# Moving the sum of the value squares to the end of its step, and halving GpSimd's subtractions

## Chip, cores and metric

One Trainium2 chip, one core. The metric is the device time of one execution in microseconds (us). Before the change it is 759.63 us, the median of 3 runs (757.01 to 761.63).

## What is computed

Attention over 8 batches, 8 heads, 576 positions and 64 values per head, then a mixture of eight experts with a fixed capacity of 576 tokens each. Heads 0 to 3 see a band of 32 positions, heads 4 to 7 see every 32nd position:

```python
scores = scale * np.matmul(q, k.transpose(0, 1, 3, 2))
mask_local = (rel >= 0) & (rel < stride)
mask_strided = (rel >= 0) & (pos[None, :] % stride == pos[:, None] % stride)
scores = np.where(masks[None, :, :, :], scores, -1000000000.0)
attn = softmax(scores)              # with 1e-09 in the divisor
x = np.matmul(attn, v)              # as 4608 tokens of 512
logits = x @ w_gate                 # each token goes to one expert, greedily, 576 per expert
out[mask] = np.maximum(x[mask] @ w1[e], 0.0) @ w2[e]
```

## The kernel before

**Stages.** The first some 260 us of the span are attention and gating, then follows a search for the assignment of tokens to the first expert, and then the eight experts, each with its gather of tokens, its weights and its scatter. The change lies in the first stage.

**Units and steps.** A batch has two units, first the strided heads, then the local ones, so unit j is batch j // 2; a unit has two pairs of heads. The program runs over steps i = -1 to 31, and the tile framework keeps each engine's instructions in the order in which the program writes them (`manual_schedule`). In step i three pairs are in work: `u` is pair i (its probabilities are multiplied by the values, `mix`, and the result is divided and scaled, `norm`), `n` is pair i + 1 (its scores are closed, its maxima are taken with `max_main` and `max_t`, then `shift` subtracts them on TensorE, line 387, and ScalarE takes the exponential, line 391), and `m` is pair i + 2 (its scores are opened). So on TensorE one step runs: close scores of n (line 364), mix of head 0 of u (408), maxima (374), mix of head 1 (408), open scores of m (353, 364), transposes of earlier results (`flip`, 482), and last the shift of n (387). I call the time from one shift to the next the length of a step.

**The scale of a batch.** The results are kept as two 16-bit halves, so each batch gets a power of two as a scale, from the sum of the squares of its values. ScalarE squares the values of a unit with a running sum per partition (`square_v`, line 299) into two columns of `vsq`. `total_v` sums them over the partitions on TensorE with a matrix of twos (line 302, 2 columns) into the small PSUM area `b`, and VectorE adds the two columns to `vsum` (304). `scale_v` makes two powers of two from it with four small VectorE instructions (`scale_of`, lines 203 to 208) and writes the exponent into the table `val` (311 and 313). `norm` of that batch needs the scale (line 429), except in the first unit, which is scaled afterwards.

**Where the sum stands.** For batches 1 to 7 total_v and scale_v are in the list `mids` of step 4b, the step whose u is the first pair of the batch's strided unit. `mids` runs between the two mixes. The square of the local unit is queued on ScalarE at the end of the step before (4b - 1), at the front of the list `fills`; the third argument of `at`, `True`, puts it there already in this kernel, ahead of `finish`. For batch 0 the sum stands in step 1 behind the norm. The list `mids3`, behind the norm and the flips, holds the logits of batch b - 2 in step 4b (line 562).

**Finish.** A pair's result x is cut into its upper half by ScalarE (line 444) and its lower half by GpSimd (x minus the upper half, line 445, both operands in SBUF), for later flips and for the stores to the scratch memory, which SyncE issues (460, 468).

```python
            def total_v(u, po):
                nc.tensor.matmul(po[:, :2], twos, vscale[u.b][0], start=True, stop=True, skip_group_check=True)
                u.vsum = wk.tile([128, 1], F32, name="vsum")
                nc.vector.tensor_reduce(u.vsum, po[:, :2], axis=AX.X, op=OP.add)
```

Of the kernel before, what the change touches and what calls it, by code (L numbers as in the profile page):

```python
# [13 lines left out]
OP = mybir.AluOpType  # L14
AX = mybir.AxisListType
# [44 lines left out]
V_BITS, W1_BITS, W2_BITS = 8, 7, 15  # L60
# [72 lines left out]
def band_stride_attention_then_capacity_moe(ctx, tc, qt, kl, ks, nl, ns, wg, w1, w2, cst, out, dbg=None):  # L133
    nc = tc.nc
# [39 lines left out]
    twos = const.tile([128, 128], F32, name="twos")  # L174
# [26 lines left out]
    def scale_of(tot, bits, pool, sc=None):  # L201
        ex = pool.tile([128, 3], I32, name="ss_e", bufs=3)
        nc.vector.tensor_single_scalar(ex[:, 2:3], tot.bitcast(I32), 24, op=OP.logical_shift_right)
        nc.vector.tensor_scalar(ex[:, 0:1], ex[:, 2:3], -1.0, float(127 + bits + 63), op0=OP.mult, op1=OP.add)
        nc.vector.tensor_scalar(ex[:, 1:2], ex[:, 2:3], 1.0, float(127 - bits - 63), op0=OP.mult, op1=OP.add)
        if sc is None:
            sc = pool.tile([128, 2], I32, name="ss_s", bufs=3)
        nc.vector.tensor_single_scalar(sc, ex[:, :2], 23, op=OP.logical_shift_left)  # L208
        return sc.bitcast(F32), ex

    def spans(b):
        n0 = b * S
        c0 = n0 // TP
        half, full = (slice(0, 64), c0 + 4) if n0 % TP == 0 else (slice(64, 128), c0)
        t0 = 0 if n0 % TP == 0 else 64
        c1 = c0 if t0 == 0 else c0 + 1
        return [(slice(0, TP), c1 + i, slice(t0 + i * TP, t0 + i * TP + TP)) for i in range(4)] + \
            [(half, full, slice(S - 64, S) if t0 == 0 else slice(0, 64))]

    with tc.tile_pool(name="ld", bufs=2) as ld, \  # L220
# [8 lines left out]
        mxb, vbuf, vscale = {}, {}, {}  # L229
# [7 lines left out]
        b = spare[:, 1, 384:]  # L237
        nc.vector.memset(po_all, 0.0)
        for i in range(2):
            for g in "sl":  # L240
                t = ld.tile([128, 32], F32, name=f"mx_{g}{i}", bufs=1)
                nc.gpsimd.memset(t, 0.0)
                mxb[g, i] = t
                t = ld.tile([128, 2, ST if g == "s" else LT, 4, VW], F32, name=f"v_{g}{i}", bufs=1)
# [29 lines left out]
        class Unit:  # L274
# [24 lines left out]
                    nc.scalar.activation(jk[r], u.vn[r, g, :, :, :D], AF.Square, accum_out=vscale[u.b][0][r, j:j + 1])  # L299

            def total_v(u, po):
                nc.tensor.matmul(po[:, :2], twos, vscale[u.b][0], start=True, stop=True, skip_group_check=True)
                u.vsum = wk.tile([128, 1], F32, name="vsum")
                nc.vector.tensor_reduce(u.vsum, po[:, :2], axis=AX.X, op=OP.add)

            def scale_v(u):
                b = u.b
                sv, ex = scale_of(u.vsum, V_BITS, wk)
                sp = spans(b)
                c = sp[0][1]  # L310
                nc.vector.tensor_scalar(val[:, 2, c:c + 4], ex[:, 1:2].to_broadcast([TP, 4]), 1.0, None, op0=OP.mult)
                r, c, _ = sp[4]
                nc.vector.tensor_scalar(val[r, 2, c:c + 1], ex[r, 1:2], 1.0, None, op0=OP.mult)
                vscale[b] = sv, None

            def load(u, parts=(slice(0, 2),), v=True):
                b, g = u.b, u.g
# [120 lines left out]
            def finish(u, p, eng):  # L438
                nr, nx = u.nr, u.nx
                if p == 0:  # L440
                    u.xo = wk.tile([128, nx, 2, 4 * D], F16, name="xo" + u.g)
                xf = u.x[:nr, :, 2 * p:2 * p + 2].rearrange("q t h d -> q t (h d)")
                c = slice(2 * D * p, 2 * D * p + 2 * D)
                nc.scalar.activation(u.xo[:nr, :, 0, c], xf, AF.Copy)  # L444
                eng.tensor_tensor(u.xo[:nr, :, 1, c], xf, u.xo[:nr, :, 0, c], op=OP.subtract)  # L445

            def store(u):
                b, xo = u.b, u.xo.rearrange("q t j d -> q t (j d)")
# [126 lines left out]
        todo = [Unit(b, strided) for b in range(B) for strided in (True, False)]  # L575
# [9 lines left out]
        mids2, mids3 = {1: todo[1]}, {GW_AT: [lambda a, b: gate_weights(b)]}  # L585
        mids, flips = {}, {}

        for j, u in enumerate(todo):
            if j == 1:
                for k in range(6):  # L590
                    drips.setdefault(k // 3, []).append(lambda u=u, k=k: u.copy_v(k))
                for p in range(2):
                    drips.setdefault(2, []).append(lambda p=p: todo[0].rescale(p))
            if j > 1:
                if not u.strided:
                    for k in range(6):
                        drips.setdefault(2 * j + COPY_AT[k], []).append(lambda u=u, k=k: u.copy_v(k))
                    at(2 * j - V_AT, u.square_v, True)
                else:
                    for f in range(2):  # L600
                        at(2 * j + 2 - V_AT_S[f], lambda u=u, f=f: u.square_v(f), j > 2)
                if not u.strided:
                    mids.setdefault(2 * j - 2, []).append(lambda a, b, u=u: (u.total_v(b), u.scale_v()))
            if not u.strided and u.b < B - 1:
                at(2 * j + (4 if u.b < B - 2 else 3), lambda k=u.b: gate_scale(k))
                if u.b < B - 2:
                    mids.setdefault(2 * j + G_AT, []).append(lambda a, b, k=u.b: gates(k, spare))
                (mids if u.b == B - 2 else mids3).setdefault(2 * j + (G_AT + 1 if u.b < B - 2 else 5), []).append(lambda a, b, k=u.b: logits(k, b))
            for p in range(2):
                at(2 * j + p if j else 2, lambda u=u, p=p: u.finish(p, nc.gpsimd))  # L610
            at(2 * j + (2 if j < nu - 2 else 1), u.store)
            if j < nu - 2:
                for p in range(2):
                    k = 2 * j + p + (2 if j else 3)
                    flips.setdefault(k, []).append((u, p))
            elif u is not todo[-1]:
                at(2 * j + 1, u.turn)
# [35 lines left out]
        def warm(i, k):  # L653
            for _ in range(WARM.get((i, k), 0)):
                nc.tensor.matmul(warm_o, warm_i[:, :128], warm_i, start=True, stop=True, skip_group_check=True)
# [5 lines left out]
        for i in range(-1, 2 * nu):  # L661
            u, n, m = pair(i), pair(i + 1), pair(i + 2)
            if i > 0 and i % 2 == 0 and i // 2 + 3 < nu:
                todo[i // 2 + 3].load()
            if n:
                close_scores(n)
            warm(i, 0)
            for f in drips.get(i, []):
                f()
            if m or i in mids:  # L670
                a = room(m) if m else ps_a.tile([128, 2, 512], F32, name="spa")
            if u:
                if u[1] == 0:
                    u[0].begin()
                if i < last:
                    u[0].mix(u[1], 0)
            if i < last:
                for f in mids.get(i, []):
                    f(a, b)
            if i == last:  # L680
                gate_scale(B - 1)
                warm(i, 1)
                pt = ps_a.tile([128, 2, 512], F32, name="spa")
                pt = pt[:, 0], pt[:, 1]
                p1 = spare[:, 0]
                for ts_, p_ in zip(parts, (None, p1)):
                    for h in range(2):
                        u[0].mix(u[1], h, ts_, p_)
                    u[0].norm(u[1], ts_, p_)
                break  # L690
            if n and MAX_FIRST:
                n[0].max_t(n[1])
            if u:
                u[0].mix(u[1], 1)
            if n and not MAX_FIRST:
                n[0].max_t(n[1])
            if i == last - 1:
                gates(B - 2, ps_a.tile([128, 2, 512], F32, name="spa"))
            warm(i, 1)
            if m:  # L700
                open_scores(m)
            warm(i, 2)
            if u:
                u[0].norm(u[1])
            for v, p in flips.get(i, []):
                v.flip(p)
                if len(flips[i]) > 1:
                    v.flipped(p)
            if i in mids2:
                mids2[i].total_v(b)  # L710
            if i == 1:
                todo[1].scale_v()
            for f in mids3.get(i, []):
                f(a, b)
            if i == -1:
                todo[0].square_v()
            if n:
                n[0].shift(n[1])
            warm(i, 3)
            if len(flips.get(i, [])) == 1:  # L720
                flips[i][0][0].flipped(flips[i][0][1])
            if i in (-1, 0):
                todo[1].square_v(i + 1)
            if i == 0:
                nc.scalar.activation(jkw, wg_sb, AF.Square, accum_out=sqw)
            for f in late.get(i, []) + fills.get(i, []):
                f()
# [659 lines left out]
```

## Time and profile before

| what | us |
|---|---|
| median of 3 runs | 759.63 (757.01 to 761.63) |
| the profiled execution's own time | 753.18 |
| its span in the profile | 751.2 |
| TensorE busy in the span | 655.4 (87%) |
| VectorE, ScalarE, GpSimd busy | 470.4, 357.1, 159.3 |

TensorE is in front, but its share is a mean over unlike stages; the profile also shows it at half clock for long stretches of the first stage. Rows of the timeline begin with the start in us from the span's start and the duration in us; then come the engine (PE is TensorE, PEld its weight loads, DVE VectorE, ACT ScalarE, POOL GpSimd, SP SyncE), the line, the operation, output and inputs, and in brackets the idle time before the row with what ended it.

### The profile page before, as it was taken

Reading aid. Unit: us, or ns where it says so; the run is one execution under the profiler, and the core shown is the slowest. Engines: PE = TensorE matmul, PEld = TensorE weight load, DVE = VectorE, ACT = ScalarE, POOL = GpSimd, SP = SyncE. Lnnn points to the kernel's source line nnn. Section 1 sums busy time; section 2 is a strip of 40 time slices with the busy share of each in tenths; the row PEclk is TensorE's granted clock in tenths of the full one; section 3 lists DMA queues with packets and bytes.
Section 4 is the critical chain, followed back from the end, with each engine's and each line's share of the span. In section 5 each row is a group of like instructions: output and inputs, shape, how many; then the busy total and the mean of one; then the engine's idle time right before and its main releaser. Section 6 shows DMA issues by size and latency. Waiting matters only on the chain.

```text
span 751.2 us, 18257 instructions
## 1 busy us (share of the span) xinstructions
PE 655.4 (87%) x7519; PEld 418.9 (56%) x7519; DVE 470.4 (63%) x1369; ACT 357.1 (48%) x548; POOL 159.3 (21%) x143
## 2 busy tenths in 40 slices
PE   5877889888698634899999999999999998899994
PEld 3555557666475532654664754764754753564752
DVE  5866676565667767796766775676775764653210
ACT  3445675554645403547527436436436335754210
POOL 9131131121212402005005004004005004112011
PEclk9668997687979856999999999999999999799998
DMA  9975575554612305419229149049049049651001
GB/s 233 261 212 129 148 205 160 159 157 135 200 33 65 77 20 195 116 48 307 61 94 289 33 141 248 26 149 252 15 166 235 15 165 242 233 125 50 15 22 42
DMA packets 75695, 102.89 MB, mean 137 GB/s; under 512 B 43020, under 2 KB 52788, under 8 KB 75100
## 3 DMA queue, kind: packets, MB, share of 16 engines
q1 hardware_dynamic: 68812, 82.23, 38.8%
q0 software_dynamic: 6080, 19.10, 8.2%
q8 instruction: 59, 0.97, 0.6%
q10 hardware_dynamic: 720, 0.39, 0.2%
q14 instruction: 24, 0.20, 0.1%
HBM read 73.59 MB, written 18.87 MB: 123 GB/s over the span
## 4 chain that ended last, share of the span: by engine, by line
PE 20%; issue 18%; DMA 8%; DVE 6%; ACT 3%; POOL 3%; SPq 2%; POOLq 0%; DVEq 0%; ACTq 0%
PE ph L1215 12%; PE ph L1263 5%; DMA w<-in_w_dram 4%; DMA xg<-x_scr,idx 2%; DVE w2l L1077 2%; POOL out_dram L1274 2%; ACT jk L1058 1%; DMA xt<-xg 1%; POOL xg L1128 1%; SPq L1131 1%; DMA out_dram<-y,idx 1%; DVE hl L1223 1%; DVE w1l L1077 1%; SPq L1043 1%; ACT w1h L1076 1%
## 5 line engine op out<-in xcount | busy, mean ns | idle before, releaser
L1215 PE MATMUL ph<-xt,w1h 128*128 128x288 f16 (+2 forms) x1024 | 181.6, 290 | 8.2 <-DMA xt<-xg 6.7
L1215 PEld LDWEIGHTS <-w1h 128*128 128x128 f16 x1024 | 97.8, 99 | 37.8 <-issue 8.2
L1274 POOL DMA_INDIRECT out_dram<-y,idx x40 | 44.0, 1099 | 339.3 <-ACT y L1273 313.9
L1215 PE MATMUL ph<-xt,w1l 128*128 128x288 f16 (+2 forms) x512 | 114.1, 290 | 0.0
L1058 ACT ACTIVATE jk<-w 128x1024 f16<-128x1024 f32 x64 | 67.4, 1053 | 72.1 <-DMA w<-in_w_dram 39.8
L1222 ACT ACTIVATE hh<-ph 128x576 f16<-128x576 f32 (+2 forms) x72 | 42.7, 594 | 122.4 <-PE ph L1215 122.3
L1263 PE MATMUL ph<-w2h,hl 128*128 128x512 f16 x256 | 97.2, 380 | 0.0
L1263 PE MATMUL ph<-w2l,hh 128*128 128x512 f16 x256 | 97.2, 380 | 0.0
L1263 PE MATMUL ph<-w2h,hh 128*128 128x512 f16 x256 | 97.2, 380 | 0.0
L1263 PEld LDWEIGHTS <-hh 128*128 128x128 f16 x512 | 48.4, 98 | 54.1 <-issue 5.0
L1223 DVE SCALAR_TENSOR_TENSOR hl<-ph,hh 128x576 f16<-128x576 f32 (+2 forms) x72 | 49.4, 687 | 44.4 <-ACT hh L1222 44.0
L391 ACT ACTIVATE pr<-spa 128x576 f32<-128x576 f32 x32 | 20.8, 650 | 92.4 <-PE spa L387 75.7
L408 PE MATMUL po<-v_s,pr 128*54 128x130 f32 (+1 forms) x384 | 54.8, 366 | 4.5 <-DMA kl<-in_kl_dram 4.0
L1215 PEld LDWEIGHTS <-w1l 128*128 128x128 f16 x512 | 50.2, 99 | 13.1 <-issue 0.6
L445 POOL TENSOR_TENSOR xos<-xs,xos 118x768 f16<-118x768 f32 x16 | 26.7, 1669 | 120.1 <-ACT xos L444 81.0
L1128 POOL DMA_INDIRECT xg<-x_scr,idx x40 | 41.2, 1029 | 50.7 <-issue 34.4
L1077 DVE SCALAR_TENSOR_TENSOR w2l<-w,w_sw,w2h 128x512 f16<-128x512 f32 x64 | 45.7, 742 | 8.7 <-ACT w2h L1076 8.5
L1077 DVE SCALAR_TENSOR_TENSOR w1l<-w,w_sw,w1h 128x512 f16<-128x512 f32 x64 | 45.5, 743 | 8.2 <-ACT w1h L1076 7.7
L1273 ACT ACTIVATE y<-ph,so 128x512 f32<-128x512 f32 x32 | 21.8, 682 | 58.1 <-PE ph L1263 40.7
L1076 ACT ACTIVATE w1h<-w,w_sw 128x512 f16<-128x512 f32 x64 | 41.8, 709 | 3.3 <-DVE w_sw L208 2.1
L1076 ACT ACTIVATE w2h<-w,w_sw 128x512 f16<-128x512 f32 x64 | 41.1, 710 | 4.3 <-DVE w_sw L208 4.3
L408 PEld LDWEIGHTS po<-v_s,pr 128*54 128x54 f32 (+1 forms) x384 | 33.3, 161 | 17.2 <-issue 15.1
(628 smaller groups left out, 1052.6 us busy)
## 6 DMA issues: line engine op xcount, KB each, us to landing
w<-in_w_dram SPq DMA_DIRECT2D x64, 512.0 KB
kl<-in_kl_dram SPq DMA_DIRECT2D x8, 608.0 KB
v_s<-in_ns_dram SPq DMA_DIRECT2D x16, 292.5 KB
v_l<-in_nl_dram SPq DMA_DIRECT2D x16, 292.5 KB
ql<-in_qt_dram SPq DMA_DIRECT2D x8, 576.0 KB
ks<-in_ks_dram SPq DMA_DIRECT2D x7, 576.0 KB
qs<-in_qt_dram SPq DMA_DIRECT2D x7, 576.0 KB
x_scr<-xol SPq DMA_DIRECT2D x28, 128.0 KB
```

The source lines that it names most:

```text
L408: nc.tensor.matmul(po[r:r + n, j:j + d + 1:d], pr[:, o:o + n], u.vn[:, :, t, 2 * p + h], start=(t < g), stop=(t + g >= u.nt), skip_group_c ...
L445: eng.tensor_tensor(u.xo[:nr, :, 1, c], xf, u.xo[:nr, :, 0, c], op=OP.subtract)
L1058: nc.scalar.activation(jk, wf[:, c * n4:(c + 1) * n4].rearrange("p c f -> p (c f)"), AF.Square, scale=1.41422, accum_out=sq[:, c:c + 1])
L1076: nc.scalar.activation(hi[:, c, f], wf[:, c, f], AF.Copy, scale=s_)
L1077: nc.vector.scalar_tensor_tensor(lo[:, c, f], wf[:, c, f], s_, hi[:, c, f], op0=OP.mult, op1=OP.subtract)
L1128: nc.gpsimd.indirect_dma_start(out=xg[:n], out_offset=None, in_=x_rows, in_offset=bass.IndirectOffsetOnAxis(ap=idx[:n, t:t + 1], axis=0))
L1215: nc.tensor.matmul(tile_[:, j, :w], wt[:, d, f * 128:(f + 1) * 128], xt[:, d // 2, xx, d % 2, c], start=(k == 0), stop=(k == 3 * DC - 1))
L1222: nc.scalar.activation(hv, src, AF.Relu)
L1223: nc.vector.scalar_tensor_tensor(lv, src, 0.0, hv, op0=OP.max, op1=OP.subtract)
L1263: nc.tensor.matmul(py, a[:, f, ts_], w[:, f], start=(k == 0), stop=(k == len(todo) - 1))
L1273: nc.scalar.activation(y, py, AF.Copy, scale=so[:, t:t + 1])
L1274: st = nc.gpsimd.indirect_dma_start(out=out_rows, out_offset=bass.IndirectOffsetOnAxis(ap=idx[:n, t:t + 1], axis=0), in_=y[:n], in_offset= ...
```

## The change

total_v and scale_v of batches 1 to 7 leave `mids` and run, for all eight batches, behind the opened scores and ahead of the norm of the same step. The two columns are summed by two accumulating one-column matmuls in place of one matmul of two columns, and VectorE copies one column where it added two. The writes to `val` become `note_v`, behind the norm. Each subtraction of `finish` is cut into two along the tiles (3 and 3 of a strided unit's six, 2 and 3 of a local unit's five). The square's place in ScalarE's queue, which the change's description names, is not in the diff.

```diff
             def total_v(u, po):
-                nc.tensor.matmul(po[:, :2], twos, vscale[u.b][0], start=True, stop=True, skip_group_check=True)
+                for k in range(2):
+                    nc.tensor.matmul(po[:, :1], twos, vscale[u.b][0][:, k:k + 1], start=(k == 0), stop=(k == 1),
+                                     skip_group_check=True)
                 u.vsum = wk.tile([128, 1], F32, name="vsum")
-                nc.vector.tensor_reduce(u.vsum, po[:, :2], axis=AX.X, op=OP.add)
+                nc.vector.tensor_copy(u.vsum, po[:, :1])
 
             def scale_v(u):
                 b = u.b
-                sv, ex = scale_of(u.vsum, V_BITS, wk)
-                sp = spans(b)
+                sv, u.ex = scale_of(u.vsum, V_BITS, wk)
+                vscale[b] = sv, None
+
+            def note_v(u):
+                ex, sp = u.ex, spans(u.b)
                 c = sp[0][1]
                 nc.vector.tensor_scalar(val[:, 2, c:c + 4], ex[:, 1:2].to_broadcast([TP, 4]), 1.0, None, op0=OP.mult)
                 r, c, _ = sp[4]
                 nc.vector.tensor_scalar(val[r, 2, c:c + 1], ex[r, 1:2], 1.0, None, op0=OP.mult)
-                vscale[b] = sv, None
...
-                eng.tensor_tensor(u.xo[:nr, :, 1, c], xf, u.xo[:nr, :, 0, c], op=OP.subtract)
+                for t in (slice(0, nx // 2), slice(nx // 2, nx)):
+                    eng.tensor_tensor(u.xo[:nr, t, 1, c], xf[:, t], u.xo[:nr, t, 0, c], op=OP.subtract)
...
                 if not u.strided:
-                    mids.setdefault(2 * j - 2, []).append(lambda a, b, u=u: (u.total_v(b), u.scale_v()))
+                    mids2[2 * j - 2] = u
...
             warm(i, 2)
+            if i in mids2:
+                mids2[i].total_v(b)
+                mids2[i].scale_v()
             if u:
                 u[0].norm(u[1])
+            if i in mids2:
+                mids2[i].note_v()
             for v, p in flips.get(i, []):
                 v.flip(p)
                 if len(flips[i]) > 1:
                     v.flipped(p)
-            if i in mids2:
-                mids2[i].total_v(b)
-            if i == 1:
-                todo[1].scale_v()
```

## Rows read from the trace of the kernel before

**Rows 1.** The page's span in 40 equal slices: TensorE's granted clock, in tenths.

```profile
PEclk9668997687979856999999999999999999799998
```

**Rows 2.** Waits of TensorE, 30 to 262 us: total us, times, longest us.

```profile
PE spare L302 <- ACT jk L299: 14.5, 7, 2.2
...
PE po L408 <- issue: 2.4, 1, 2.4
...
PE spa L364 <- issue: 2.0, 1, 2.0
```

**Rows 3.** Timeline of batch 3's sum step, all engines.

```profile
105.02 0.41 PE L387 MATMUL spa<-dd,sel 128*128 128x288 bf16 x2
...
107.40 2.12 ACT L299 ACTIVATE jk<-v_l 64x2304 f16<-64x2304 f32 x1
...
109.66 0.38 PE L302 MATMUL spare<-vsq,twos 128*128 128x2 f32 x2 [2.25 <-ACT jk L299]
...
110.45 1.40 POOL L445 TENSOR_TENSOR xol<-xl,xol 128x640 f16<-128x640 f32 x1 [6.82 <-ACT xol L444]
...
110.72 1.15 DVE L208 TENSOR_SCALAR ss_s<-ss_e 128x2 int32<-128x2 int32 x1
...
113.21 0.22 DVE L429 TENSOR_SCALAR rc<-po,ss_s 118x12 f32<-118x12 f32 x1
...
113.80 0.96 DVE L432 TENSOR_TENSOR xs<-po,rc 118x768 f32<-118x768 f32 x1
...
116.22 0.42 PE L387 MATMUL spa<-dd,sel 128*128 128x288 bf16 x1
```

**Rows 4.** Stretches of 2 us of that step: busy time, granted clock, DMA share, GB/s.

```profile
108.00:110.00 2.00, 0.34 (x6) 0.32 (x6) 0.07 (x1) 1.98 (x3) 0.00 (x0) 1.00 0.95 251
...
114.00:116.00 2.00, 2.00 (x11) 1.91 (x11) 0.76 (x1) 0.00 (x0) 0.00 (x0) 0.50 0.33 105
```

**Rows 5.** Timeline: shifts that begin and end batch 2's steps.

```profile
78.74 0.41 PE L387 MATMUL spa<-dd,sel 128*128 128x288 bf16 x2
...
94.82 0.42 PE L387 MATMUL spa<-dd,sel 128*128 128x288 bf16 x2
...
99.23 0.40 PE L387 MATMUL spa<-dd,sel 128*128 128x288 bf16 x2
```

**Rows 6.** Timeline around the end of batch 7's sum step, at full clock.

```profile
238.90 0.28 PE L562 MATMUL spare<-sum_g,lt 128*128 128x8 f32 x1
...
240.10 0.42 PE L387 MATMUL spa<-dd,sel 128*128 128x288 bf16 x2
...
241.31 0.32 PE L408 MATMUL po<-v_s,pr 128*54 128x130 f32 x2
...
244.51 0.29 PE L482 MATMUL spare<-ident_h,xol 128*128 128x128 f16 x2
...
245.43 0.42 PE L387 MATMUL spa<-dd,sel 128*128 128x288 bf16 x2
```

**Rows 7.** Timeline of batch 0's sum, in step 1, and the next step's first mix.

```profile
30.41 0.38 PE L302 MATMUL spare<-vsq,twos 128*128 128x2 f32 x2
...
31.65 0.17 DVE L208 TENSOR_SCALAR ss_s<-ss_e 128x2 int32<-128x2 int32 x1
...
31.82 0.32 PE L408 MATMUL po<-v_l,pr 128*32 128x130 f32 x4
```

**Rows 8.** Line 445's instructions: minimum, median and maximum ns, first and last start.

```profile
L445 POOL TENSOR_TENSOR xos<-xs,xos x16: 1640/1646/1965, 38.3 to 248.4; 118x768 f16<-118x768 f32 x16
L445 POOL TENSOR_TENSOR xol<-xl,xol x16: 1388/1396/1737, 41.9 to 259.9; 128x640 f16<-128x640 f32 x16
```

**Rows 9.** Timeline: VectorE beside the second of two GpSimd subtractions back to back.

```profile
40.69 1.25 DVE L379 CAST mh<-mr 128x32 bf16<-128x32 f32 x1
...
41.86 1.39 POOL L445 TENSOR_TENSOR xol<-xl,xol 128x640 f16<-128x640 f32 x1
...
41.97 1.33 DVE L380 TENSOR_TENSOR mh<-mr,mh 64x32 bf16<-64x32 f32 x1
```

## The prediction, made before the changed kernel was run

> **What bounds the kernel now.** I read the page's slices first, then TensorE's waits, then the timeline step by step. The slices show TensorE's granted clock falling to about six tenths again and again in the first fourteen slices, which are attention, and staying high over the experts [rows 1]. So TensorE is the busiest engine there and yet does not get its full clock. The list of its waits in this stage has one line that stands far above the rest: seven waits of the sum's matmul (line 302) for ScalarE's square, 14.5 us together, 2.2 us at most [rows 2]. One per batch, 1 to 7.
>
> Batch 3's sum step shows why. The step begins with the shift at 105.02. ScalarE starts the square at 107.40 and needs 2.12 us for it; TensorE stands from the end of the first mix until 109.66, 4.64 us into the step, and behind the sum in its queue stand the maxima, the second mix, the opened scores, the transposes, the logits and the next shift, none of which needs the sum except through VectorE [rows 3]. In the 2 us with the wait TensorE is busy for 0.34 us and still has full clock; soon after it runs at 0.50, that is at 1.2 in place of 2.4 GHz, and is busy all the time [rows 4]. The step takes 11.20 us from shift to shift [rows 3]. The wait therefore costs twice: by itself, and by the slow clock behind it, which lasts into the next step. In this stage TensorE's order is the path to the end: the search needs the last batch's logits, and the experts need the search, so what a step loses the end loses.
>
> **What the change removes.** I compare the stretch from the shift at 78.74 (start of batch 2's sum step) to that at 240.10 (end of batch 7's): 161.36 us, six sum steps and five each of the three others of a batch [rows 5, 6]. What the others take at full clock can be read: behind a sum step 5.33 us (240.10 to 245.43), then 4.41 (94.82 to 99.23), then 5.79 (99.23 to 105.02) [rows 3, 5, 6], in all 15.53.
>
> A sum step without the early wait: in the step behind batch 7's, which has the same sequence on TensorE, the transposes start 4.41 us after the shift [rows 6]. That is the sum's new place. The square is done 4.64 us after the shift, as before, since nothing ahead of it on ScalarE changes [rows 3]. So a wait of 0.23 us is left. Then comes the sum. One matmul of two columns took 0.38 us [rows 3]; a second one of one column is not in the trace, and costs between nothing (a load of the same weights hidden behind the first) and 0.38. I take 0.38, as most of it is the weight load, which does not shrink with the columns; 0.76 together. Then the transposes, 0.92 to the shift behind them, and the logits, 1.20 to theirs [rows 6]. Sum: 4.64 + 0.76 + 0.92 + 1.20 = 7.52 us, in place of 11.20 in batch 3.
>
> So the stretch becomes 6 x 7.52 + 5 x 15.53 = 122.8 us. To that I add 5 us for two waits of TensorE for its own issue, 2.4 and 2.0 us [rows 2], which fall into two of the other steps and have nothing to do with the sum, with a little slow clock behind. 161.4 - 127.8 = **33.6 us gained**. Batch 1's sum step starts at a low clock for another reason and waits less; I count nothing for it.
>
> **What it moves to VectorE.** The copy for the sum now stands behind the maxima and ahead of the norm, so the norm waits for the sum, and the next step's first mix, which overwrites the PSUM that the norm reads, waits for the norm. The cover is the transposes, the logits, the shift and the next close of scores. From the sum's start to the shift instruction of the scale (line 208) it is 1.06 us; with the second matmul that instruction is ready 4.64 + 1.06 + 0.38 = 6.08 us into the step. Before, it lay 1.15 us beside GpSimd's subtraction, which began 5.43 us into the step [rows 3]; undisturbed it takes 0.17 [rows 7]. The norm takes 1.55 us, from 113.21 to the end of the row at 113.80 [rows 3]. That ends at about 7.8 us, and the next first mix comes at 7.52 + 1.21 = 8.73 [rows 6]. Hidden, with 0.9 us to spare. The copy for the two-column addition costs the same, and the two writes to val, now behind the norm, are in nobody's way. The moved instructions issue no DMA; ScalarE's and SyncE's queues keep their order.
>
> In batch 0 the cover is missing: step 1 has neither transposes nor logits. There the sum stood behind the norm. Now the scale is ready at 30.41 + 0.38 + 1.06 + 0.17 = 32.0 and the norm ends 1.55 later, at 33.6, while the next mix, at 31.82 before, would come at 32.2 [rows 3, 7]. That is a new wait of 1.4 us, and 0.4 for the second matmul: **1.8 us lost**, once.
>
> **What halving GpSimd's subtractions does.** 768 elements took 1646 ns and 640 took 1396, so 1.95 ns per element and 146 ns per instruction [rows 8]. 32 more instructions are 4.7 us on GpSimd, which is idle for most of the stage; its results are needed a step later. By the Trainium skill (GPSIMD Engine Reference, section 3.1), which has a two-input subtraction at about 2.6 cycles per element of a 1.2 GHz clock, I estimate 1.66 us for 768 elements, which leaves no fixed share, and by it halving would be free. The rows' 146 ns decide. What matters more is VectorE beside them: some of its instructions stand still while GpSimd subtracts. Between two subtractions back to back one waiting VectorE instruction, the cast, got in after 1.25 us, but the next one then waited 1.33 us for the second [rows 9]. So halving helps where one instruction waits, as line 208 does: GpSimd's first piece, of 256 elements (0.65 us), ends at 6.08, just as line 208 is ready. It does not help a chain of two or three, like the maxima's, which then waits for both pieces and for the extra 0.15 us. From both sides: a gain of 3 us, if the sum's chain mattered; a loss of 4.7, if every added instruction lay on the path. I take 1 us lost, nearer to nothing, as the maxima's chain sets the shift in a few steps only.
>
> **The sum**: 33.6 - 1.8 - 1.0 = 30.8 us. The profiled execution took 753.18 us, so it would take 722.4; the median of the runs is 6.45 higher, and I take the same off it: 759.63 - 30.8 = **729 us**.
>
> **Rivals.**
> First, only the waits go and the clock falls all the same, because something else in these steps lets it. For it: the clock also fell in slices ahead of the first long wait [rows 1]. Against: the rows tie this fall to the wait [rows 4], and batch 2's other steps ran at full clock with waits of under a microsecond. Gain 14.5 - 7 x 0.38 - 2.8 = 9 us: 751. Chance 0.10.
>
> Second, the two waits for issue multiply. Faster steps pull the same loads and stores into less time, and if the instructions themselves come by the same DMA engines, which were at 0.95 in the sum step [rows 4], each remaining batch may get such a wait of 2.2 us: four more, 9 us, 738. The rows give no cause for them, only "issue" [rows 2]. Chance 0.12. The Trainium skill (Runtime: NRT & Kernel Launch, section Instruction fetch mechanics) holds fetching to be mostly hidden behind the issue of instructions; by that this rival would not come, and no row here shows which it is.
>
> Third, on the other side: the wait comes back at the next step's first mix, with VectorE's chain as the bound. It has 0.9 us to spare. It decides once the chain is longer by that and by the 2.2 us removed. If it made TensorE stand for 2.4 us there, with the clock falling as now, each of seven batches would lose 2.4 + 0.38 - 2.24 = 0.5 us, and with the 2.8 of batch 0 and GpSimd the time is 766. For it: batch 0 shows the mechanism, 1.4 us [rows 7]. Against: the chain would have to grow by 3 us, and even with line 208 held for both pieces (to 5.43 + 1.55 = 7.0 us) it grows by 0.9. Chance 0.05.
>
> Fourth, the sum still waits for the square as long as now. The square's place is named in the description and not in the diff; if TensorE reached the sum as early as before, nothing would change: 760. But between the first mix and the sum's new place lie the maxima, a mix and the opened scores. Chance 0.04.
>
> **How the numbers follow.** My forecast has 0.69. Its own bounds, the second matmul from nothing to 0.38 (3 us), GpSimd's 3 gained to 4.7 lost, and a clock that differs between runs, give 720 to 737. The second rival lies at 738 and up to 746 with slow clock behind each wait; with it the range 718 to 746 holds 0.81. A measurement of this kernel can tell about 0.5%, 3.8 us. Faster by more: 0.69 + 0.10 + 0.12 = 0.91. Same: 0.04. Slower: 0.05.
>
> **What would show it.** Right: line 302 has twice the instructions and almost no wait for the square; TensorE's clock stays full over steps 8 to 29; sum steps near 7.5 us; line 208 takes under 0.4 us; the logits of the last batch come some 31 us earlier and everything behind moves with them, unchanged. Wrong: the first mix of the step behind a sum waiting for the norm in batches 2 to 7; half clock between sums; more waits for issue; the maxima's chain holding the shift in most steps.

## The result, and the profile after

The changed kernel takes **730.54 us** (median of 4 runs, 726.02 to 733.75) against 759.45 of the kernel before on the same chip: a ratio of 0.9616, 95% interval 0.9549 to 0.9682. The forecast was 729, the range 718 to 746. (A ratio leaves disturbed runs out, so it need not be the quotient of two medians; kernels that ran on different chips are compared below by their ratios alone.) The profiled execution took 728.22 us, 24.96 less than that of before.

The page of the changed kernel: its span, the engines' busy time, and the granted clock by slices.

```profile
span 726.2 us, 18338 instructions
...
PE 643.6 (89%) x7535; PEld 412.2 (57%) x7535; DVE 460.8 (63%) x1369; ACT 357.9 (49%) x548; POOL 165.4 (23%) x175
...
PEclk8887999989987569999999999999999998899998
```

Attention ends a little over one slice earlier, and the sixes that stood among its slices [rows 1] are gone: it has sevens, eights and nines. The clock is better, but it isn't full: the sevens and eights are spread over the stage.

TensorE's waits of the changed kernel, 30 to 262 us, as in [rows 2] (those from 235 us on belong to the search).

```profile
PE spa L391 <- DVE dd L386: 4.3, 3, 1.6
...
PE spare L487 <- ACT lt L521: 2.4, 4, 0.7
PE spa L368 <- issue: 2.3, 1, 2.3
...
PE spare L487 <- DVE vsum L306: 1.7, 7, 0.3
...
PE po L412 <- DVE xs L436: 1.2, 1, 1.2
```

The 14.5 us for ScalarE's square are gone; no wait of the sum's matmuls is left in the list. Two waits are new, and both are small: the transposes (line 487) wait for VectorE's copy of the sum (line 306), 0.25 us in each of seven batches, and one mix waits 1.2 us for the norm, which is batch 0's. There is one issue wait in place of two.

The timeline of batch 2's sum step and the step behind it, the changed kernel.

```profile
73.68 0.41 PE L391 MATMUL spa<-dd,sel 128*128 128x288 bf16 x2
...
74.88 1.09 PE L412 MATMUL po<-v_s,pr 128*54 128x130 f32 x11
...
76.06 2.12 ACT L299 ACTIVATE jk<-v_l 64x2304 f16<-64x2304 f32 x1
...
78.09 0.62 PE L303 MATMUL spare<-vsq,twos 128*128 128x1 f32 x4
...
78.75 0.16 DVE L306 COPY vsum<-spare 128x1 f32<-128x1 f32 x1 [0.95 <-PE spare L303]
...
78.96 0.98 PE L487 MATMUL spare<-ident_h,xol 128*128 128x128 f16 x10 [0.25 <-DVE vsum L306]
79.11 1.54 POOL L450 TENSOR_TENSOR xol<-xl,xol 128x256 f16<-128x256 f32 x2 [7.49 <-ACT xol L448]
79.38 0.43 DVE L208 TENSOR_SCALAR ss_s<-ss_e 128x2 int32<-128x2 int32 x1
...
80.44 0.96 DVE L436 TENSOR_TENSOR xs<-po,rc 118x768 f32<-118x768 f32 x1
81.07 0.42 PE L391 MATMUL spa<-dd,sel 128*128 128x288 bf16 x2
...
82.28 1.81 PE L412 MATMUL po<-v_s,pr 128*54 128x130 f32 x11
```

The sum starts 4.41 us into the step, just when the square ends, and the step takes 7.39 us, where batch 3's took 11.20 [rows 3]. The norm ends at 81.40, 0.88 us before the next first mix, which waits for nothing. But that mix needs 1.81 us for eleven matmuls; a step earlier, at 74.88, eleven of the same took 1.09. The stretches of 2 us say why: busy time of PE, PEld, DVE, ACT and POOL, granted clock, DMA share and GB/s.

```profile
78.00:80.00 2.00, 1.75 (x27) 1.35 (x20) 1.11 (x6) 1.01 (x3) 0.89 (x2) 1.00 0.69 273
80.00:82.00 2.00, 2.00 (x52) 1.72 (x53) 1.55 (x7) 0.42 (x1) 0.65 (x1) 1.00 0.16 45
82.00:84.00 2.00, 2.00 (x42) 1.58 (x35) 1.21 (x2) 2.00 (x3) 0.00 (x0) 0.60 0.27 88
84.00:86.00 2.00, 2.00 (x21) 1.47 (x14) 1.06 (x4) 1.43 (x3) 0.49 (x1) 0.55 0.61 125
86.00:88.00 2.00, 2.00 (x39) 1.22 (x39) 1.41 (x3) 0.00 (x0) 1.38 (x2) 1.00 0.56 158
```

Full clock through the sum, the transposes and the logits, then some 3.5 us at half of it, then full again, with no wait above 0.25 us in the 13 us ahead of it. The step behind the sum therefore takes 6.91 us (81.07 to 87.98) and not the 5.33 of [rows 6].

Line 208 and GpSimd's pieces, minimum, median and maximum ns (line 208 up to 262 us).

```profile
L208 DVE TENSOR_SCALAR ss_s<-ss_e x9: 169/428/432, 30.6 to 204.1; 128x2 int32<-128x2 int32 x9
```

```profile
L450 POOL TENSOR_TENSOR xos<-xs,xos x32: 906/919/1232, 38.3 to 217.9; 118x384 f16<-118x384 f32 x32
L450 POOL TENSOR_TENSOR xol<-xl,xol x32: 667/796/1234, 42.4 to 228.4; 128x256 f16<-128x256 f32 x16, 128x384 f16<-128x384 f32 x16
```

Batch 0's sum and the next step's mixes.

```profile
29.30 0.61 PE L303 MATMUL spare<-vsq,twos 128*128 128x1 f32 x4
...
31.11 0.96 DVE L436 TENSOR_TENSOR xs<-po,rc 118x768 f32<-118x768 f32 x1
32.17 0.65 PE L412 MATMUL po<-v_l,pr 128*32 128x130 f32 x16 [1.17 <-DVE xs L436]
```

**Where the time went.** GpSimd's first reduction of the search marks the end of attention in each profile: 267.81 before, 235.38 after, so the stage is 32.4 us shorter. What follows it took 483.4 us before and 490.8 after. Of the 32.4 us only 25.0 are left in these two executions; whether something takes the rest back is tested below.

### The profile page after: what moved, and what is told of

Read it like the earlier page. It is cut to its first block, busy times and chain, and to the rows that moved or that the text cites. A ratio compares the mean times of both kernels' runs of the same rounds, so it can differ in the third digit from the quotient of the medians.

```text
span 726.2 us, 18338 instructions
## 1 busy us (share of the span) xinstructions
PE 643.6 (89%) x7535; PEld 412.2 (57%) x7535; DVE 460.8 (63%) x1369; ACT 357.9 (49%) x548; POOL 165.4 (23%) x175
## 4 chain that ended last, share of the span: by engine, by line
PE 25%; issue 17%; DMA 12%; DVE 5%; POOL 3%; SPq 3%; ACT 1%; POOLq 0%; DVEq 0%; ACTq 0%
PE ph L1221 18%; DMA xg<-x_scr,idx 5%; DMA w<-in_w_dram 4%; PE ph L1269 3%; SPq L1137 2%; DMA xt<-xg 2%; POOL xg L1134 2%; DVE w2l L1083 2%; POOL out_dram L1280 1%; PE ph L1263 1%; DVE hl L1229 1%; SPq L1049 1%; ACT jk L1064 1%; PE ph L1122 0%; DVE y L1277 0%
## 5 line engine op out<-in xcount | busy, mean ns | idle before, releaser
L1221 PE MATMUL ph<-xt,w1h 128*128 128x288 f16 (+2 forms) x1024 | 183.8, 292 | 13.5 <-DMA xt<-xg 11.1
L412 PE MATMUL po<-v_s,pr 128*54 128x130 f32 (+1 forms) x384 | 49.9, 343 | 4.5 <-ACT pr L395 3.8
L450 POOL TENSOR_TENSOR xos<-xs,xos 118x384 f16<-118x384 f32 x32 | 29.9, 955 | 89.8 <-ACT xos L448 69.1
L1269 PEld LDWEIGHTS <-hl 128*128 128x128 f16 x256 | 25.0, 98 | 26.2 <-issue 0.6
```

Source lines behind the costliest of these rows:

```text
L412: nc.tensor.matmul(po[r:r + n, j:j + d + 1:d], pr[:, o:o + n], u.vn[:, :, t, 2 * p + h], start=(t < g), stop=(t + g >= u.nt), skip_group_c ...
L450: eng.tensor_tensor(u.xo[:nr, t, 1, c], xf[:, t], u.xo[:nr, t, 0, c], op=OP.subtract)
L1221: nc.tensor.matmul(tile_[:, j, :w], wt[:, d, f * 128:(f + 1) * 128], xt[:, d // 2, xx, d % 2, c], start=(k == 0), stop=(k == 3 * DC - 1))
L1269: nc.tensor.matmul(py, a[:, f, ts_], w[:, f], start=(k == 0), stop=(k == len(todo) - 1))
```

## The experiments

Theories: **the clock** (the wait costs little by itself, the half clock behind it most), against **the wait alone**; and for the parts, that the move is everything, against a share of the halved subtractions, the two matmuls or the square's place.

### The parts one by one

The first four ran on one chip (the kernel before: 757.26 us). The move alone: the changed kernel with whole subtractions and one matmul.

```diff
-                for t in (slice(0, nx // 2), slice(nx // 2, nx)):
-                    eng.tensor_tensor(u.xo[:nr, t, 1, c], xf[:, t], u.xo[:nr, t, 0, c], op=OP.subtract)
+                eng.tensor_tensor(u.xo[:nr, :, 1, c], xf, u.xo[:nr, :, 0, c], op=OP.subtract)
...
-                for k in range(2):
-                    nc.tensor.matmul(po[:, :1], twos, vscale[u.b][0][:, k:k + 1], start=(k == 0), stop=(k == 1),
-                                     skip_group_check=True)
+                nc.tensor.matmul(po[:, :2], twos, vscale[u.b][0], start=True, stop=True, skip_group_check=True)
                 u.vsum = wk.tile([128, 1], F32, name="vsum")
-                nc.vector.tensor_copy(u.vsum, po[:, :1])
+                nc.vector.tensor_reduce(u.vsum, po[:, :2], axis=AX.X, op=OP.add)
```

> The changed kernel without the halved subtractions and with one matmul of two columns and the addition: the move alone. Theory: TensorE's wait for the square and the half clock behind it were the cost, so the move alone gives nearly all of the gain: 728 to 735 us, sum steps of 7.3 to 7.6 us from shift to shift, line 208 again near 1.1 us but the next first mix waiting at most 0.3 us for the norm. Rival (VectorE held up by GpSimd is the cost, and the halves pay): line 208 at 1.1 us pushes the norm past the next mix in every batch, sum steps or the steps behind them are 0.8 us longer or more, and the time is 737 us or more.

Measured: 730.86 us, ratio 0.9628 (0.9571 to 0.9684). The move alone gives the whole gain. Line 208 then stands still for GpSimd again, and that costs nothing that these runs can tell:

```profile
L208 DVE TENSOR_SCALAR ss_s<-ss_e x9: 168/1154/1159, 30.1 to 207.8; 128x2 int32<-128x2 int32 x9
```

The halves alone, in the kernel before:

```diff
-                eng.tensor_tensor(u.xo[:nr, :, 1, c], xf, u.xo[:nr, :, 0, c], op=OP.subtract)
+                for t in (slice(0, nx // 2), slice(nx // 2, nx)):
+                    eng.tensor_tensor(u.xo[:nr, t, 1, c], xf[:, t], u.xo[:nr, t, 0, c], op=OP.subtract)
```

> The kernel before with the halved subtractions alone. Theory: nothing that sets the end waits for one VectorE instruction beside GpSimd alone, so within 0.5% of the kernel before (756 to 763 us), with the seven waits for the square still 14 to 15 us. Rival (the halves pay): at least 6 us faster, 753 us or less, as line 208 and the maxima's chain wait for half as long.

Measured: 755.93 us, ratio 0.9976 (0.9939 to 1.0014): nothing that can be told from no change. The wait for the square stays:

```profile
PE spare L302 <- ACT jk L299: 15.6, 7, 2.2
```

In the same kernel line 208's median falls from 1064 (1154 at most) to 380 ns, so the halves do shorten VectorE's block, and the time doesn't show it.

The changed kernel with whole subtractions (the diff above, reversed), both matmuls kept:

> The changed kernel with whole subtractions: the move and the two matmuls. Theory: within 3 us of the changed kernel (728 to 734); the norm ends 0.8 us later and just about meets the next first mix, so that mix waits 0 to 0.3 us. Rival (the halves pay): 736 us or more.

Measured: 730.0 us, ratio 0.9622 (0.9569 to 0.9675). The changed kernel with halves and one matmul in place of two (the second part of the first diff):

> The changed kernel with one matmul of two columns and the addition in the new place. By the sum of the prediction the second matmul costs up to 0.38 us in eight steps, so 0 to 3 us faster than the changed kernel (726 to 731). Rival: the two matmuls let the first column go ahead before the square of the second is done, so that one matmul waits 0.2 us for the square and nothing is gained: sum steps the same 7.4 us. A third point to read: the changed kernel's clock still falls for 3.4 us behind most sum steps; if the four weight loads of the two matmuls do that, it goes away here and the steps behind a sum step fall from 6.8 to 5.3 us (some 8 us faster).

Measured: 726.42 us, ratio 0.9573 (0.952 to 0.9626). All three kernels with the move lie between 0.957 and 0.963 with overlapping intervals, so neither the halves nor the second matmul has a price that these runs can tell from nothing. With one matmul the sum waits a little for the square again, 0.17 us in each of six batches, which the first of the two matmuls, with a column that is long ready, doesn't:

```profile
PE spare L302 <- ACT jk L299: 1.0, 6, 0.2
```

So the sum steps stay at 7.38 to 7.52 us in five batches of six (7.70 in the last), as the rival had it. And the steps behind them took 5.33 us in two batches and 6.89 to 8.27 in four: the weight loads of the second matmul alone are not what lets the clock fall there.

### Filling the wait

This one decides between the clock and the wait. In the kernel before, nine matmuls that nothing reads are put ahead of each of the seven sums. TensorE then reaches the sum no earlier, and the sum leaves no earlier; all that changes is that it works where it stood still.

```diff
-                    mids.setdefault(2 * j - 2, []).append(lambda a, b, u=u: (u.total_v(b), u.scale_v()))
+                    mids.setdefault(2 * j - 2, []).append(lambda a, b, u=u: (fill(9), u.total_v(b), u.scale_v()))
```

```diff
+        def fill(n):
+            for _ in range(n):
+                nc.tensor.matmul(warm_o, warm_i[:, :128], warm_i, start=True, stop=True, skip_group_check=True)
```

> The kernel before with nine idle matmuls (128x512, results not used) ahead of each sum in its old place, so that TensorE works while it waits for the square; the wait stays as long. Theory (the wait costs twice, by itself and by the half clock behind it): the clock stays full behind the sums, sum steps go from 10.7 to 12.5 down to 9.2 to 9.7 us and the steps behind them from up to 8 to 5.3 us, 18 to 24 us faster than the kernel before: 735 to 741 us. Rival (the clock falls for another reason, the wait alone is what the change removes): sum steps stay over 10.5 us and the time within 0.5% of before.

Measured, on another chip (the kernel before: 752.22 us): 728.53 us, ratio 0.9726 (0.9667 to 0.9784), so 2.74% of 752.22 = **20.6 us** (16.2 to 25.1), from work that does nothing. By the wait alone it would have been nought. The absolute figures of the expectation were for the first chip. Timeline and stretches of 2 us of its batch 2:

```profile
78.01 2.12 ACT L299 ACTIVATE jk<-v_l 64x2304 f16<-64x2304 f32 x1
78.04 2.10 PE L659 MATMUL spare<-warm_i 128*128 128x512 bf16 x9
...
80.28 0.38 PE L302 MATMUL spare<-vsq,twos 128*128 128x2 f32 x2
...
84.93 0.42 PE L387 MATMUL spa<-dd,sel 128*128 128x288 bf16 x2
```

```profile
78.00:80.00 2.00, 2.00 (x10) 0.82 (x9) 0.68 (x2) 1.99 (x1) 0.00 (x0) 1.00 0.93 375
...
82.00:84.00 2.00, 2.00 (x40) 1.43 (x39) 1.86 (x9) 0.00 (x0) 0.46 (x1) 1.00 0.04 6
84.00:86.00 2.00, 2.00 (x60) 1.72 (x59) 1.20 (x4) 0.57 (x2) 0.00 (x0) 1.00 0.26 76
```

Its sum steps of batches 2 to 7 take 9.29 or 9.30 us each, 1.9 more than the 7.39 of the changed kernel; the sum still leaves 4.64 us into the step. Before, they took 10.74 to 12.48. The Trainium skill (TensorE: Matmul & The Clock Gate, section HAM oscillation) describes a kernel that waits for data after each short burst of matmuls and pays for the clock at every one; this kernel did that once per batch, with waits of 2.2 us.

### The square's place

Two ways to let the square end at another time. Early: in the kernel before, the local unit's square one step ahead (and one copy of the values moved with it), the sum left in its old place.

```diff
-V_AT, V_AT_S, COPY_AT = 3, (6, 5), (-2, -4, -2, -4, -1, -3)
+V_AT, V_AT_S, COPY_AT = 4, (6, 5), (-2, -4, -2, -4, -1, -4)
```

> The kernel before with the local square one step earlier, at the end of step 4b-2, and its last copied third on VectorE one step earlier too; the sum stays between the mixes. Theory (the wait is the cost and not the place): no wait for the square, sum steps of 6.8 to 7.3 us, no fall of the clock behind them; the square now stands ahead of the copies of gate scores on ScalarE in step 4b-1, which grows from 5.8 to 7 to 8 us; 728 to 742 us. Rival (the sum in the middle of the step holds TensorE up by VectorE or by its own place): sum steps of 9 us or more, 745 us or more.

Measured: 733.81 us, ratio 0.9734 (0.9684 to 0.9783). The sum doesn't wait any more, and the sum steps of batches 2 and 5 take 7.00 us; those of the other four take 9.7 to 10.4. The wait went to another place, a step earlier. TensorE's waits and stretches of 2 us of this kernel:

```profile
PE spare L482 <- ACT lt L516: 14.2, 6, 2.7
```

```profile
98.00:100.00 2.00, 0.13 (x3) 0.13 (x3) 0.32 (x1) 1.81 (x2) 1.40 (x1) 1.00 0.43 122
...
102.00:104.00 2.00, 2.00 (x14) 1.23 (x10) 1.50 (x3) 1.53 (x3) 0.37 (x1) 0.50 0.92 222
```

ScalarE's copy of the gate scores (`lt`, from which the logits are made) now stands behind the square, the transposes wait 14.2 us for it in six batches, TensorE is busy for 0.13 of 2 us, and the clock falls into the sum step. It is the same mechanism with another wait.

Late: the changed kernel, with the square behind `finish` in ScalarE's queue.

```diff
-                    at(2 * j - V_AT, u.square_v, True)
+                    at(2 * j - V_AT, u.square_v)
```

> The changed kernel with the local square behind the copy of finish in ScalarE's queue, 0.74 us later. Theory: the sum, which comes 4.41 us behind the shift, now waits some 0.6 us for the second column in each of batches 1 to 7, so sum steps of 7.9 to 8.2 us and 733 to 738 us. Rival (0.7 us is hidden behind something): sum steps stay at 7.4 us and the time at 728 to 732.

Measured: 736.92 us, ratio 0.9801 (0.9758 to 0.9844). Of TensorE's waits:

```profile
PE spare L303 <- ACT jk L299: 4.1, 7, 0.6
```

The waits come back in small, the sum steps take 8.1 to 9.1 us, and attention ends at 243.11 in place of 235.38. The square in front is needed for the whole gain, but the kernel before had it there already.

### The slow clock that is left

The logits leave the sum step: they run one step later for batches 0 to 5.

```diff
-                (mids if u.b == B - 2 else mids3).setdefault(2 * j + (G_AT + 1 if u.b < B - 2 else 5), []).append(lambda a, b, k=u.b: logits(k, b))
+                (mids if u.b == B - 2 else mids3).setdefault(2 * j + (G_AT + 2 if u.b < B - 2 else 5), []).append(lambda a, b, k=u.b: logits(k, b))
```

> The changed kernel with the logits of batches 0 to 5 one step later, so that they no longer stand in the sum step. Theory (the clock's short fall behind the sum steps comes from the stretch of sum, transposes and logits, which are mostly weight loads): the fall goes away in most batches, sum steps of 6.2 us, the steps behind them 6.4 to 6.6 us at full clock, and 722 to 727 us. Rival (the two matmuls of the sum alone let it fall): the falls stay, the steps behind take 8 us or more, and the time stays within 3 us of 730.

Measured: 726.21 us, ratio 0.9677 (0.9617 to 0.9736). Stretches of 2 us of its batch 2, whose step behind the sum runs from 76.65 to 83.62:

```profile
78.00:80.00 2.00, 1.68 (x28) 1.43 (x29) 1.72 (x7) 2.00 (x2) 0.00 (x0) 1.00 0.26 73
80.00:82.00 2.00, 2.00 (x40) 1.18 (x37) 1.86 (x6) 1.01 (x3) 0.91 (x2) 1.00 0.42 105
82.00:84.00 2.00, 2.00 (x22) 1.58 (x21) 0.46 (x3) 0.00 (x0) 0.88 (x2) 1.00 0.98 260
```

Full clock all the way. The sum steps are 6.18 or 6.19 us and the steps behind 6.97 to 6.99, with the logits in them (7.16 in the last): 13.2 for both, where the changed kernel has 14.2 to 15.6 in five of six batches. The steps behind are longer than the 6.4 to 6.6 of the expectation because the first mix now waits 0.42 us for the norm, which ends at 78.18 (the bracket names the write to `val` right behind it); the logits were a part of the norm's cover:

```profile
77.22 0.96 DVE L436 TENSOR_TENSOR xs<-po,rc 118x768 f32<-118x768 f32 x1
...
78.32 1.06 PE L412 MATMUL po<-v_s,pr 128*54 128x130 f32 x11 [0.42 <-DVE val L318]
```

So the fall right behind a sum step goes away when the logits leave the row of sum, transposes and logits, and no long wait is needed for it. What lets the clock fall there is not settled: batch 6 of the changed kernel has the same row and no fall (5.33 us behind it), and here the clock fell one step further on in three later batches (5.6 to 7.0 us in place of 4.41). Attention ends at 228.51, 6.9 us earlier than in the changed kernel, yet the time is no better by its ratio.

### Does the rest of the kernel take it back?

The last four ran on one chip (the kernel before: 759.64 us, with runs from 751.75 to 765.21). The changed kernel itself again:

> The changed kernel once more, as the partner of the three others on one chip. Both theories: a ratio of 0.955 to 0.969 to the kernel before. In its first profile the attention stage ended 32.4 us earlier than before, but the rest of the span was 7.4 us longer (490.8 against 483.4). If the longer rest is chance of a profiled execution, the rest may lie anywhere between 483 and 493 this time; if it belongs to an attention stage that ends early, it is 489 to 493 again.

Measured: 725.60 us (720.72 to 731.70), ratio 0.9562 (0.9507 to 0.9617). Its profiled execution was the slowest of its six, 731.70, with attention ending at 234.98 and 494.7 us behind it, more than either theory had. Now with attention held back by filling in step 28:

```diff
+            if i == 28:
+                fill(32)
             warm(i, 2)
```

> The changed kernel with 32 matmuls of 512 columns that nothing reads on TensorE in step 28, behind the last sum's step, at 0.21 us each (1.90 us for nine, from the kernel with the filled wait): the attention stage ends 6.8 us later and nothing else is touched. Theory 'the end follows the end of attention, and what the expert stage takes on top is chance': the median is 5 to 9 us above the changed kernel's on this chip. Theory 'the expert stage gives back what an earlier start gains, because something in it keeps a pace of its own': the median is at most 3 us above, and the rest of the span behind attention is shorter than the changed kernel's.

Measured: 734.66 us, ratio 0.9692 (0.9638 to 0.9746), 9.1 us above the changed kernel by medians and 1.30% of 759.64 = 9.9 by ratios. The timeline of that step:

```profile
197.49 0.41 PE L391 MATMUL spa<-dd,sel 128*128 128x288 bf16 x2
...
201.89 7.08 PE L664 MATMUL spare<-warm_i 128*128 128x512 bf16 x32
...
211.67 0.42 PE L391 MATMUL spa<-dd,sel 128*128 128x288 bf16 x2
```

The step takes 14.18 us, against 7.73 and 7.48 in the two profiles of the changed kernel: some 6.6 us of delay. All of it is in the time, and a little more, by ratios that are each uncertain by some 4 us. What is lost in the attention stage comes through, and the rival, at most 3 us, falls. That leaves open why the part behind attention is longer with the move; more on it at the end of the next section.

Last, two attempts at something better. One matmul, and batch 0's sum behind its norm as before the change:

```diff
-            if i in mids2:
+            if i in mids2 and i > 1:
                 mids2[i].total_v(b)
                 mids2[i].scale_v()
             if u:
                 u[0].norm(u[1])
+            if i == 1:
+                mids2[i].total_v(b)
+                mids2[i].scale_v()
```

> The changed kernel with one matmul of two columns, and batch 0's sum behind its norm, as before the change. Theory 'batch 0 loses its cover': the wait of step 2's first mix for the norm (1.17 us) is gone, steps 0 to 2 together 1.0 to 1.8 us shorter than with one matmul alone (6.37 + 6.31 or so for the first two there). With the one matmul's fewer falls of the clock the median is 2 to 6 us below the changed kernel's. Rival 'step 1 is bound by something else': the wait moves to another instruction and nothing is gained over one matmul alone.

Measured: 729.31 us, ratio 0.9468 (0.9381 to 0.9555); the ratio rests on the two lowest of its six runs, which lie between 713.48 and 734.99, so far apart that I don't rank it. (The expectation speaks of steps 0 to 2; step 0 ends ahead of the edit and took from 11.3 to 13.4 us in these profiles, so I compare steps 1 to 3.) The timeline of step 2:

```profile
28.25 0.40 PE L389 MATMUL spa<-dd,sel 128*128 128x288 bf16 x2
...
30.50 0.65 PE L410 MATMUL po<-v_l,pr 128*32 128x130 f32 x15 [0.59 <-issue]
...
34.38 0.41 PE L389 MATMUL spa<-dd,sel 128*128 128x288 bf16 x2 [1.48 <-DVE dd L384]
```

The mix no longer waits for the norm, but the shift waits 1.48 us for VectorE's maxima: step 2 takes 6.13 us, 0.32 less than in the changed kernel. Steps 1 to 3 together are 1.5 us shorter than with one matmul alone (17.4 against 18.9), but 1.2 of that is step 1, which took from 4.9 to 7.6 us in these profiles, and from 4.9 to 7.5 in those that leave batch 0's sum as it was before. So this edit buys 0.3 us: the wait moved, as the rival said.

And with the logits one step later as well:

> As the kernel before it in this list, with the logits of batches 0 to 5 one step later. Attention should end at 226 to 229 us, 6 to 9 us earlier than in the changed kernel, because the sum step is 6.2 us and the step behind it 7.0 without the slow clock. Theory 'chance': the median is 6 to 10 us below the changed kernel's. Theory 'given back': it stays within 3 us of the kernel with the first sum behind, and the rest of the span behind attention is 494 to 497 us.

Measured: 724.84 us, ratio 0.9556 (0.9509 to 0.9604), like the changed kernel's 0.9562. In its profile the sum steps are 6.18 or 6.19 us, but attention ended at 236.00 and not at 226 to 229: it has issue waits of 2.7 and 1.7 us, and the clock fell again behind 150 us. I found no version that is shown to beat the changed kernel.

## Why the prediction was right

The mechanism was right, and so was the forecast of the time, but that it came within 2 us is in part luck: several terms were off, in both directions, and the part behind attention did not stay unchanged.

**The wait costs twice.** Right, and shown apart: with the wait filled, the clock alone is worth some 20.6 us.

**Sum steps of 7.52 us.** Measured 7.38 to 7.39 in four batches of six, 7.50 and 7.73 in two. The wait of 0.23 for the square didn't come: the sum starts 4.41 us into the step, not 4.64. The second matmul added 0.24 us (0.62 for both against 0.38), where I had taken 0.38. What I had not seen is the transposes' wait for the copy, 0.25. The errors cancel.

**The other steps at full clock.** This is the step that failed: "5.33 us" for the step behind a sum. In the stretch from the shift at 73.68 to that at 206.15 they took 6.91, 6.81, 6.79, 8.09 and 5.33, together 7.3 us more than forecast. I had taken 5.33 from behind batch 7's sum step, whose sum stood far ahead of its logits. With sum, transposes and logits in one row the clock fell in five batches of six without a long wait. "TensorE's clock stays full over steps 8 to 29" was wrong with it. The end of the stretch and the step behind it, in the changed kernel:

```profile
206.15 0.66 PE L391 MATMUL spa<-dd,sel 128*128 128x288 bf16 x2
214.06 0.42 PE L391 MATMUL spa<-dd,sel 128*128 128x288 bf16 x2
```

**The stretch.** 161.36 us became 132.5, not 127.8: 28.9 gained, not 33.6. Of the 4.7 between, 7.3 are the steps behind; back come 2.25 because one issue wait cost 2.75 where I had left 5 for two, and 0.35 from the sum steps.

**Batch 1, counted at nothing.** Its sum step went from 14.19 to 10.01 us. Everything ahead of 78.74 became 5.06 us shorter, with batch 0's loss inside. This covers the shortfall of the stretch. Behind 206.15 the next step took 7.91 us in place of 5.33 [rows 6]. In all, 28.9 + 5.1 - 1.5 = 32.4 us, and I had forecast 30.8 with other terms.

**Batch 0.** The new wait was forecast at 1.4 and is 1.17; step 2 grew by 0.96 us (5.49 to 6.45), not 1.8. The experiment shows why so little: without this wait another one, for the maxima, has most of it.

**VectorE's chain.** The norm's end was forecast 7.8 us into the step and is 7.72; the spare 0.9, and it is 0.88. The third rival didn't come. Nor did it when line 208 took 1154 ns again; with the logits a step later a small form of it did, 0.42 us in each of six batches. Line 208 was forecast under 0.4 us and took 0.43.

**The halves.** Forecast at 1 us lost; nothing was found in either direction, which the bounds held. GpSimd's busy time grew by 6.1 us (159.3 to 165.4), not by 4.7: 0.19 us per instruction, where [rows 8] gave 146 ns. Two pieces of 384 elements take 2 x 0.919 us where the whole took 1.646 [rows 8], so the fixed share is real. The Trainium skill (GPSIMD Engine Reference, section 3.1) was set against this there; by its 2.6 cycles per element of a 1.2 GHz clock 384 elements would take, as an estimate, 0.83 us, less than the row's 0.919.

**The other rivals.** That the clock falls all the same came true in part: 7.3 us in the stretch, where some 22 would have made 751. The issue waits didn't multiply in the changed kernel (one of 2.3); in the others with the move they came to between 0.7 and 5.1 us in an execution (without the 1.17 at batch 0's mix that some of these traces put down to issue; that mix starts when the norm ends). The traces show where they stand: between 40 us and the end of attention all 24 issue waits of over 0.3 us in the fourteen profiles come behind 1488, 1996, 2376, 2629 or 2883 matmuls of TensorE, whichever instruction is next. So they belong to the place in the stream of instructions and not to what a step does. The Trainium skill (Runtime: NRT & Kernel Launch, section Instruction fetch mechanics) was cited for their not coming; no run here shows whether fetching is what they are. The fourth rival is out.

**From the stage to the time.** 32.4 us in the stage, 25.0 in the two profiled executions, but 28.9 by the medians of the first comparison and 34.0 by those of the second (759.64 to 725.60). The profiled execution of before was 6.27 us faster than the median of its chip (759.45), so it flattered what comes behind attention. One thing stays open: in the ten profiles with the move the part behind attention took 490.4 to 496.1 us, in the four without it 483.4 to 486.6. It doesn't follow the time at which attention ends: with the wait filled that was 240.32, with 486.2 behind it, and in the delayed kernel 239.96, with 491.8. The ratios of one chip point the same way: attention ended 4.7 us earlier with the square behind (243.11) than with the early square (247.80), and yet its ratio is the higher one (0.9801 against 0.9734). A part of it stands at the start of the experts, where TensorE waits for the gathered tokens, 7.1 to 13.5 us with the move and 5.8 to 8.9 without. So the move seems to cost some 7 us behind attention, by the means of the profiles; I have no cause for it.

## What to carry to other kernels

Where TensorE waits a couple of microseconds once in each round, look at its granted clock behind the wait before pricing it: here 2.2 us of waiting cost over 4 per batch (32.4 over seven), and filling them with empty work recovered 20.6 us of 752. A wait that is moved to another place in the same queue (the early square) takes its clock with it. And after such a wait is gone, read the steps behind again: a duration taken from a step with another order of matmuls doesn't hold for the clock.

## What the hardware showed that was not expected

The clock can fall without a long wait: two passes over a sum, ten transposes and ten logit matmuls in one row, TensorE busy for 1.75 and 2.00 us of 2 us, and from 82 us on a granted clock of 0.60 and 0.55. With the logits a step later the same batch kept 1.00; but so did batch 6 with the row as it was, so the row alone doesn't decide it.

A transpose waited for VectorE's copy out of another part of the same PSUM tile, 0.25 us in each of seven batches; nothing in the trace of before shows such a wait for the sum. No run tells whether the chip asks for it or the semaphores that the program sets.

Between GpSimd's two pieces a waiting VectorE instruction gets in: line 208 took 0.43 us beside them, 1.15 beside the whole, 0.17 alone. The Trainium skill (SBUF — State Buffer, section Who interferes with whom) has it that one of the two engines blocks until the other's instruction has ended; the trace agrees, and cutting the instruction shortened the block, but not the kernel.
